# Second products of a convolution and two-layer MLP kernel: the two 64-row halves issued in opposite phase

## The chip, the cores and the metric

The kernel runs on one core of a Trainium2 chip. The metric is the device time of one execution in microseconds, lower is better; a number given as the time of a kernel is the median of several runs.

## What is computed

A dynamic convolution (each of 8 heads mixes 7 neighbouring tokens with softmax weights) makes 16384 tokens of 192 values. They go through an MLP with a squared ReLU:

```python
h = x @ w_in                 # (16384, 192) @ (192, 2048)
r = np.maximum(h, 0.0)
g = s * (r * r) + b
return (g @ w_out)           # (16384, 2048) @ (2048, 192)
```

The kernel is held to float32 inputs and outputs. It splits each operand of a product into a high part that TensorE multiplies exactly (type `fp32r`) and a low part, and adds up the products hi x hi, hi x lo and lo x hi.

## The kernel before

The tokens are cut into 32 groups of 512 (`g`), the 2048 hidden units into four quads of four 128-unit blocks (`k`), so there are 128 stages `n = 4 g + k`. Each stage has first products (`h = x @ w_in` for one quad, into the PSUM tiles `ph`), a squared ReLU on ScalarE (`relu2`: L443, L445, and L449 which writes the high part `gh`), the low part `gl` on VectorE (`low_g`, L455), and second products (`g @ w_out`, into the four PSUM tiles `po`, one for each 128 tokens). ScalarE and VectorE work on stage n while TensorE runs the second products of stage n-1, and VectorE also does the convolution of a later group. When the four quads of a group are summed, VectorE scales the result (L512, L518) and SyncE stores it.

The first four stages run while the weights are still being prepared, and use matmuls over all 128 rows (`mm1_pair`, L408 and L414; `mm2_pair`, L482). From then on every matmul uses 64 rows: `HALVES` (L378) are rows 0 to 63 and 64 to 127 of the contraction, each on one half of the array, with their own weights, so that two matmuls run beside each other. First products are in `mm1_quad` (L432), 36 matmuls of 512 columns a stage. Second products are in `mm2_quad` (L500), 64 matmuls a stage, called 123 times.

In a second product the stationary operand (the weights that are loaded into the array) is 128 tokens of `gh` or `gl`, and the moving one is a row block of `w_out`. With `part` 0 (`gh`) it is w_out's high and low part side by side, 384 columns; with `part` 1 (`gl`) it is the high part alone, 192 columns, added onto the second half of the same PSUM tile (`second`, the two `return dict` lines). `mm2_quad` takes four steps (`at`); in a step the first half of the rows adds to one `po` tile and the second half to another (`first`), so that the halves never write one tile at the same time. Within a step the loop over `c` runs over two 256-unit pairs (`p`), the two blocks in each (`j`) and the two parts, and the innermost loop over the halves:

```python
for c in range(8):
    p, j, part = c // 4, c // 2 % 2, c % 2
    for i, rows in enumerate(HALVES):
        m = second(n, p, j, first[i], part, rows)
```

So both halves are at their 384-column matmul together, then both at their 192-column matmul. The order of a queue is the order of the program (`tc.manual_schedule()`); nothing is reordered by a planner. After each of the first two steps `hand_over` puts a no-op of GpSimd behind the two tiles.

Of the kernel before, what the change touches and what calls it, by code (L numbers as in the profile page):

```python
# [20 lines left out]
def dynamic_conv_then_relu2_mlp(  # L21
# [44 lines left out]
    NQ = M // QUAD  # L66
# [170 lines left out]
    def w2(i, j, rows=slice(0, P)):  # L237

        return wc[i][rows, :, CO + j * D:CO + (j + 1) * D]
# [138 lines left out]
    HALVES = slice(0, 64), slice(64, P)  # L378
# [5 lines left out]
    def hand_over(*sums):  # L384


        for o in sums:
            nc.gpsimd.keepalive_nop(ins=[nc.gpsimd.lower_ap(o)])
# [69 lines left out]
    def outputs(g):  # L458
        o_t[g] = [ps_o.tile([P, 2, D], F32, tag=f"o{t}", name="po") for t in range(NT)]
        y_t[g] = yp.tile([P, NT, D], F32, tag="y", name="y")  # L460

    def second(n, p, j, t, part, rows=slice(0, P)):

        g, k = divmod(n, NQ)
        o, w = o_t[g][t], w2(2 * k + p, j, rows)
        v = g_t[n, p][part][rows, j, t * P:(t + 1) * P]
        start = part == 0 and (g, t) not in begun
        begun.add((g, t))
        if part == 0:
            return dict(out=o, lhsT=v, rhs=w, start=start, stop=False)  # L470
        return dict(out=o[:, 1, :], lhsT=v, rhs=w[:, 0, :], start=False, stop=False)
# [14 lines left out]
    def mm2_quad(n):  # L486


        g, k = divmod(n, NQ)
        if g not in o_t:  # L490
            outputs(g)
        turn = [(0, 2), (2, 0)][::1 - n % 2 * 2]
        for at in range(4):
            first = [a + at % 2 for a in turn[at // 2]]
            for c in range(8):
                p, j, part = c // 4, c // 2 % 2, c % 2
                for i, rows in enumerate(HALVES):
                    m = second(n, p, j, first[i], part, rows)
                    m["stop"] = k == NQ - 1 and at >= 2 and c == 7
                    nc.tensor.matmul(**m)  # L500
            if at < 2:
                hand_over(*[o_t[g][t] for t in first])
        for p in range(2):
            g_t.pop((n, p))
# [29 lines left out]
    with tc.manual_schedule():  # L534
# [22 lines left out]
        for i in range(NC):  # L557
            n, p = divmod(i, 2)
# [25 lines left out]
        for n in range(NQ, last + 1):  # L584
            g, k = divmod(n, NQ)
            if k == 0 and g + 2 < NG:
                load(g + 2)
            if k == 3:
                zeros_before(g + 2)
            mm1_quad(n)  # L590
            relu2(n)
            if n == NQ:
                mm2_pair(n - 1, 1)
            else:
                mm2_quad(n - 1)
            a = (3, 5), (5, 8), (9, 14), (0, 2)
            run_pieces(g + 1 + k // 3, *a[k])
            low_g(n, 0)
            if k == 0:
                scale(g - 1, (0, 2, 1, 3))  # L600
                store(g - 1, 0, NT)
            low_g(n, 1)
            a = (5, 5), (8, 9), (14, 15), (2, 3)
            run_pieces(g + 1 + k // 3, *a[k])
# [36 lines left out]
```

## Time and profile before

| what | value |
|---|---|
| time, median of 3 runs | 1181.46 us (1181.32 to 1181.98) |
| span of the profiled execution (first to last instruction) | 1178.3 us |
| median of the runs less that span | 3.2 us |
| TensorE matmul / weight load busy | 97% / 88% |
| VectorE / ScalarE / GpSimd busy | 80% / 70% / 1% |
| DMA, mean over the span | 43 GB/s |

The profile is of one execution. PE is TensorE's matmul row, PEld its weight loads, DVE is VectorE, ACT ScalarE, POOL GpSimd, SP SyncE. Ends of matmuls are modelled and matmuls overlap, so the time that one takes is read from the distance between starts. Stretches are in microseconds from the start of the span. The profiled execution's own time outside its span is not recorded; the runs' median stands for it in the table.

### The profile page before, as it was taken

Reading aid. Unit: us, or ns where it says so; the run is one execution under the profiler, and the core shown is the slowest. Engines: PE = TensorE matmul, PEld = TensorE weight load, DVE = VectorE, ACT = ScalarE, POOL = GpSimd, SP = SyncE. Lnnn points to the kernel's source line nnn. Section 1 sums busy time; section 2 is a strip of 40 time slices with the busy share of each in tenths; the row PEclk is TensorE's granted clock in tenths of the full one; section 3 lists DMA queues with packets and bytes.
Section 4 is the critical chain, followed back from the end, with each engine's and each line's share of the span. In section 5 each row is a group of like instructions: output and inputs, shape, how many; then the busy total and the mean of one; then the engine's idle time right before and its main releaser. Section 6 shows DMA issues by size and latency. Waiting matters only on the chain.

```text
span 1178.3 us, 29855 instructions
## 1 busy us (share of the span) xinstructions
PE 1144.9 (97%) x12672; PEld 1034.5 (88%) x12672; DVE 938.2 (80%) x1357; ACT 826.4 (70%) x889; POOL 6.1 (1%) x22
## 2 busy tenths in 40 slices
PE   2999999999999999999999999999999999999997
PEld 1678999999999999999999999999999999999997
DVE  7988887788887778887778898777788777888843
ACT  2767767777677677776776776767767677677674
POOL 0000000000000000000000000000000000000000
PEclk9999999999999999999999999999999999999999
DMA  7421222221122222122222112222112222212110
GB/s 155 117 44 28 40 46 47 32 46 27 35 46 46 39 40 37 30 40 47 46 33 46 26 36 46 46 35 44 29 37 42 47 46 33 45 26 36 24 24 14
DMA packets 175833, 50.17 MB, mean 43 GB/s; under 512 B 165076, under 2 KB 168660, under 8 KB 175700
## 3 DMA queue, kind: packets, MB, share of 16 engines
q1 hardware_dynamic: 172820, 47.73, 22.6%
q8 instruction: 99, 1.62, 0.6%
q10 hardware_dynamic: 2880, 0.54, 0.3%
q14 instruction: 34, 0.28, 0.1%
HBM read 27.26 MB, written 12.58 MB: 34 GB/s over the span
## 4 chain that ended last, share of the span: by engine, by line
PE 95%; DVE 2%; ACT 1%; DMA 1%; SPq 0%; issue 0%
PE po L500 47%; PE ph L432 43%; PE po L482 2%; PE ph L219 1%; PE ph L408 1%; DVE pr L300 1%; PE ph L414 1%; DMA r<-in_moe_w_in_dram 0%; DVE gl L455 0%; DVE pr L311 0%; ACT gh L449 0%; PE ph L246 0%; ACT r L445 0%; SPq L101 0%; DMA xb<-xb 0%
## 5 line engine op out<-in xcount | busy, mean ns | idle before, releaser
L500 PE MATMUL po<-wc,gh 64*128 64x384 f32 x3936 | 570.5, 356 | 0.0
L500 PE MATMUL po<-wc,gl 64*128 64x192 f32 x3936 | 492.8, 247 | 0.8 <-DVE gl L455 0.8
L455 DVE TENSOR_TENSOR gl<-r,gh 128x1024 fp32r<-128x1024 f32 x256 | 313.1, 1223 | 213.1 <-ACT gh L449 206.9
L443 ACT ACTIVATE r<-ph 128x1024 f32<-128x1024 f32 x256 | 249.0, 1024 | 300.0 <-PE ph L432 295.1
L500 PEld LDWEIGHTS po<-wc,gl 64*128 64x128 f32 x3936 | 375.7, 188 | 6.3 <-DVE gl L455 1.1
L500 PEld LDWEIGHTS po<-wc,gh 64*128 64x128 f32 x3936 | 368.7, 184 | 5.1
L432 PE MATMUL ph<-xa,wc 64*128 64x512 f32 x2976 | 365.6, 391 | 0.0
L432 PEld LDWEIGHTS ph<-xa,wc 64*128 64x128 f32 x2976 | 269.8, 184 | 52.9 <-issue 0.2
L449 ACT CAST gh<-r 128x1024 fp32r<-128x1024 f32 x256 | 269.2, 1052 | 7.9
L445 ACT ACTIVATE r<-r 128x1024 f32<-128x1024 f32 x256 | 270.7, 1057 | 0.3
L300 DVE TENSOR_TENSOR pr<-xt,w 128x1152 f32<-128x1152 f32 (+1 forms) x128 | 193.6, 1554 | 2.5 <-DMA r<-in_moe_w_in_dram 0.7
L432 PE MATMUL ph<-xb,wc 64*128 64x512 f32 x1488 | 190.4, 388 | 0.0
L432 PEld LDWEIGHTS ph<-xb,wc 64*128 64x128 f32 x1488 | 139.9, 184 | 30.5
L311 DVE TENSOR_TENSOR pr<-pr 128x768 f32<-128x768 f32 (+1 forms) x128 | 145.2, 1155 | 2.1
L512 DVE SCALAR_TENSOR_TENSOR u<-po,s_sb,bias 128x192 f32<-128x192 f32 x128 | 49.8, 410 | 1.6 <-PE po L482 1.6
L518 DVE SCALAR_TENSOR_TENSOR y<-po,s_sb,u 128x192 f32<-128x192 f32 x128 | 49.8, 409 | 0.1
L219 PE MATMUL ph<-r,eye_f 128*128 128x384 f32 x32 | 15.6, 570 | 18.2 <-DVE r L198 18.2
L319 DVE TENSOR_TENSOR acc<-pr 128x768 f32<-128x768 f32 x32 | 30.6, 958 | 1.1
L330 DVE STREAM_TRANSPOSE xT<-acc 128x128 f32<-128x128 f32 x128 | 28.5, 280 | 1.1
L335 DVE STREAM_TRANSPOSE xT<-acc 128x128 f32<-128x128 f32 x128 | 27.2, 271 | 0.0
L482 PE MATMUL po<-wc,gh 128*128 128x384 f32 x80 | 23.9, 361 | 0.1
L219 PEld LDWEIGHTS ph<-r,eye_f 128*128 128x128 f32 x32 | 5.7, 205 | 20.8 <-issue 20.8
(45 smaller groups left out, 336.0 us busy)
## 6 DMA issues: line engine op xcount, KB each, us to landing
xt<-in_x_dram SPq DMA_DIRECT2D x120, 132.0 KB, 3.4
out_dram<-y SPq DMA_DIRECT2D x128, 96.0 KB, 1.9
xb<-xb SPq DMA_DIRECT2D x128, 64.0 KB
wg<-in_weight_gen_dram SPq DMA_DIRECT2D x128, 28.0 KB, 2.6
r<-in_moe_w_out_dram SPq DMA_DIRECT2D x8, 384.0 KB, 3.7
r<-in_moe_w_in_dram SPq DMA_DIRECT2D x16, 128.0 KB, 3.0
r<-in_moe_w_in_dram SPq DMA_DIRECT2D x32, 32.0 KB, 2.2
xt<-in_x_dram ACTq DMA_DIRECT2D x4, 132.0 KB, 4.0
```

What stands on the lines that cost most here:

```text
L219: nc.tensor.matmul(out=o, lhsT=eye_f, rhs=fv[:, c], start=True, stop=False)
L300: nc.vector.tensor_tensor(out=pr[:, k0:k1, :, h * G:(h + 1) * G], in0=bass.AP(xs.tensor, xs.offset, [xs.ap[0], [FQ, n], [FQ, J], [1, G]]), ...
L311: nc.vector.tensor_tensor(out=pr[:, o:o + n], in0=pr[:, o:o + n], in1=pr[:, a:a + n], op=ALU.add)
L432: nc.tensor.matmul(out=h_t[n, p][:, j], lhsT=w1(2 * k + p, part, block, j, rows), rhs=v[rows], start=(at < 2 and c == 0), stop=(at >= 4 an ...
L443: nc.scalar.activation(out=r[p], in_=h_t.pop((n, p)), func=AF.Relu)
L445: nc.scalar.activation(out=r[p], in_=r[p], func=AF.Square)
L449: nc.scalar.copy(out=gh, in_=r[p])
L455: nc.vector.tensor_tensor(out=gl, in0=sq, in1=gh.bitcast(F32), op=ALU.subtract)
L482: nc.tensor.matmul(**m)
L500: nc.tensor.matmul(**m)
L512: nc.vector.scalar_tensor_tensor(out=u[i], in0=o_t[g][tiles[i]][:, 1, :], scalar=s_sb, in1=bias, op0=ALU.mult, op1=ALU.add,)
L518: nc.vector.scalar_tensor_tensor(out=y[:, t], in0=o_t[g][t][:, 0, :], scalar=s_sb, in1=u[i - 1], op0=ALU.mult, op1=ALU.add,)
```

## The change

In `mm2_quad` the loop over `c` goes over the four blocks (`p`, `j`), and the four matmuls of a block are written out with their half `i` and their `part`. Before, their order was half 0 part 0, half 1 part 0, half 0 part 1, half 1 part 1. After, it is half 0 part 0, half 1 part 1, half 1 part 0, half 0 part 1, so that each half has 384 columns while the other has 192. Where a sum is begun (`opens`: the first quad of a group, steps 0 and 1, block 0) the old order is kept, since the 384-column matmul has to clear the PSUM tile first. `stop` marks the last matmul of each half in the new order.

```diff
-            for c in range(8):
-                p, j, part = c // 4, c // 2 % 2, c % 2
-                for i, rows in enumerate(HALVES):
-                    m = second(n, p, j, first[i], part, rows)
-                    m["stop"] = k == NQ - 1 and at >= 2 and c == 7
+            opens = k == 0 and at < 2
+            for c in range(4):
+                p, j = c // 2, c % 2
+                for i, part in ((0, 0), (1, 1), (1, 0), (0, 1)) if c or not opens else ((0, 0), (1, 0), (0, 1), (1, 1)):
+                    m = second(n, p, j, first[i], part, HALVES[i])
+                    m["stop"] = k == NQ - 1 and at >= 2 and c == 3 and part == 1 - i
                     nc.tensor.matmul(**m)
```

## Rows read from the trace of the kernel before

**Rows 1.** Page, engine totals (busy us, share of the span, instructions) and L500's groups

```profile
PE 1144.9 (97%) x12672; PEld 1034.5 (88%) x12672; DVE 938.2 (80%) x1357; ACT 826.4 (70%) x889; POOL 6.1 (1%) x22
...
L500 PE MATMUL po<-wc,gh 64*128 64x384 f32 x3936 | 570.5, 356 | 0.0
L500 PE MATMUL po<-wc,gl 64*128 64x192 f32 x3936 | 492.8, 247 | 0.8 <-DVE gl L455 0.8
```

**Rows 2.** Page, chain that ended last: share of the span by engine, by line

```profile
PE 95%; DVE 2%; ACT 1%; DMA 1%; SPq 0%; issue 0%
PE po L500 47%; PE ph L432 43%; PE po L482 2%; PE ph L219 1%; PE ph L408 1%; DVE pr L300 1%; PE ph L414 1%; DMA r<-in_moe_w_in_dram 0%; DVE gl L455 0%; DVE pr L311 0%; ACT gh L449 0%; PE ph L246 0%; ACT r L445 0%; SPq L101 0%; DMA xb<-xb 0%
```

**Rows 3.** Waits of PE: waiter <- releaser, us in total, times, longest

```profile
PE po L482 <- DVE gl L455: 1.7, 2, 0.9
...
PE po L500 <- DVE gl L455: 0.8, 1, 0.8
```

**Rows 4.** Stage table: stretch, length, busy us (instructions) by engine, granted clock, DMA

```profile
599.67:603.83 4.16, 4.16 (x42) 3.41 (x39) 3.29 (x6) 2.49 (x4) 0.00 (x0) 1.00 0.04 6
603.83:608.39 4.56, 4.56 (x67) 4.56 (x64) 1.05 (x1) 4.50 (x6) 0.00 (x0) 1.00 0.42 63
```

**Rows 5.** Timeline, PE, one quad's second products (start us, length us, operation, count)

```profile
603.83 0.34 PE L500 MATMUL po<-wc,gh 64*128 64x384 f32 x2
604.00 0.25 PE L500 MATMUL po<-wc,gl 64*128 64x192 f32 x2
604.09 0.36 PE L500 MATMUL po<-wc,gh 64*128 64x384 f32 x2
604.29 0.25 PE L500 MATMUL po<-wc,gl 64*128 64x192 f32 x2
604.38 0.36 PE L500 MATMUL po<-wc,gh 64*128 64x384 f32 x2
...
608.10 0.36 PE L500 MATMUL po<-wc,gh 64*128 64x384 f32 x2
608.30 0.25 PE L500 MATMUL po<-wc,gl 64*128 64x192 f32 x2
608.39 1.11 PE L432 MATMUL ph<-xa,wc 64*128 64x512 f32 x8
```

**Rows 6.** Timeline, PEld, start of the same quad

```profile
604.00 0.19 PEld L500 LDWEIGHTS po<-wc,gh 64*128 64x128 f32 x2
604.11 0.19 PEld L500 LDWEIGHTS po<-wc,gl 64*128 64x128 f32 x2
604.29 0.19 PEld L500 LDWEIGHTS po<-wc,gh 64*128 64x128 f32 x2
604.40 0.19 PEld L500 LDWEIGHTS po<-wc,gl 64*128 64x128 f32 x2
604.58 0.19 PEld L500 LDWEIGHTS po<-wc,gh 64*128 64x128 f32 x2
604.69 0.19 PEld L500 LDWEIGHTS po<-wc,gl 64*128 64x128 f32 x2
```

**Rows 7.** Timeline, PE, after the last quad

```profile
1166.56 0.44 PE L482 MATMUL po<-wc,gh 128*128 128x384 f32 x1
1166.84 0.25 PE L482 MATMUL po<-wc,gl 128*128 128x192 f32 x1
```

**Rows 8.** Timeline, PEld, the same place (in brackets: idle before, releaser)

```profile
1166.56 0.19 PEld L482 LDWEIGHTS po<-wc,gh 128*128 128x128 f32 x1 [0.16 <-ACT r L445]
```

**Rows 9.** Timeline, PE, first phase, second products over all 128 rows

```profile
48.62 0.36 PE L482 MATMUL po<-wc,gh 128*128 128x384 f32 x1
48.82 0.25 PE L482 MATMUL po<-wc,gl 128*128 128x192 f32 x1
48.91 0.36 PE L482 MATMUL po<-wc,gh 128*128 128x384 f32 x1
...
50.34 0.36 PE L482 MATMUL po<-wc,gh 128*128 128x384 f32 x1
```

**Rows 10.** Timeline, PE, the wait in the first quad

```profile
98.72 0.36 PE L500 MATMUL po<-wc,gl 64*128 64x192 f32 x2 [0.83 <-DVE gl L455]
```

## The prediction

> **What bounds the kernel now.** I read the page's engine totals first: TensorE's matmul row is busy 97% of the span and no other computing engine passes 80% [rows 1]. The chain that ended last is TensorE for 95%, and one line, the second products of L500, carries 47% of it [rows 2]. The waits of the matmul row show that little is lost to other engines there: L500 waited once, 0.8 us, for a `gl` [rows 3]. So the question is how fast TensorE gets through L500's own stream. The stage table has a regular beat: 4.16 us of first products, 4.56 us of second products, at granted clock 1.00 [rows 4]. There are 123 quads of second products (3936 matmuls of each width, 32 of each a quad [rows 1]), so 123 x 4.56 = 561 us hang on the change.
>
> **One period, read from starts.** Durations of single matmuls overlap, so I go by starts. A row "x2" holds the two halves, which start within 0.01 us of each other (the merged row is as long as one matmul). In a quad the 384-column pairs start at 604.09, 604.38, ... 608.10: 14 periods in 4.01 us, 0.2865 us each [rows 5]. In one of them the 192-column pair starts 0.20 after the 384-column pair, and the next 384-column pair 0.085 after that (0.08 or 0.09 in the rows). But the first 384-column pair, whose weights had been loaded long before, is followed after only 0.17 (603.83 to 604.00), and the first period takes 0.26 (603.83 to 604.09). So about 0.0265 us of every later period is not streaming.
>
> The weight loads say what it is [rows 6]. In the steady quad a half's load starts with its 192-column matmul (604.00, 604.29, 604.58), and its next load 0.11 later (604.11, 604.40, 604.69), although the 384-column matmul between them is taken up already 0.085 after the first load began. So a load occupies its half for 0.11 us (its recorded length, 0.19, is longer than the distance to the next one, so I go by starts here too); the 192-column matmul covers only 0.085 of it, and the 384-column matmul behind it gets its weights 0.025 late. The same is seen where nothing covers a load: after an idle gap at 1166.56 a load and its 384-column matmul have the same recorded start, and the next matmul follows 0.28 later, 0.11 of load and 0.17 of streaming [rows 7, 8]. A matmul's recorded start is therefore when it is taken up, not when its weights are in.
>
> Decisive for the change is whether this stall belongs to each half by itself or to both together, through a common load path. Both halves' loads run side by side and take 0.11 [rows 6]; and in the first phase, where one 128-row matmul has the array to itself (L482), the period is the same: 48.62 to 50.34, six periods in 1.72 us, 0.287 [rows 9]. One load at a time buys nothing there. So I take the stall to be private: in each half, a 384-column matmul behind a 192-column one waits for its own load.
>
> **The change part by part.** Nothing is added or removed: 64 matmuls and 64 loads a quad, 32 of each width, same operands, and the two halves write different PSUM tiles before and after. Only the order of issue moves: of each four, first half 384, second half 192, second half 384, first half 192. No DMA and no other engine's instruction is moved past. Each half still alternates 384 and 192, so each still has one badly covered load a period.
>
> I follow both halves from the start of the first half's 384 at time 0, by the lengths above. Second half: its 192 also at 0; the load for its 384 starts with that and is in at 0.11; its 384 streams until 0.287 (0.176 long behind a late load: 0.2865 - 0.11). First half: its 192 at 0.176, where the next load starts; that is in at 0.287, and the next 384 streams from there. The second half's next 192 needs a load that stands behind the first half's in the program: issued just after 0.176, in at 0.287, which is just when its 384 ends. Period 0.287 for both, as before: 123 x 16 = 1968 periods x (0.2865 - 0.2865) = 0.
>
> That tie is the first unseen cost: the second half's 192 may come some ns late. It then trails and is tied no longer, so the cost falls once a quad, not once a period. No row shows unequal matmuls side by side; what the rows show of a 384 in two surroundings is 0.176 (late load) against 0.17, so I let up to 0.004 us a period stand in doubt either way, 1968 x 0.004 = 8 us. I take 0, by the row of the lone stream [rows 9], which is nearest to two halves that don't touch each other, and keep -8 and +8.
>
> The border of a quad is the second. Before, both halves end on a 192. After, the first half ends on its 192 at 0.26 and the second on its 384 at 0.287; the 512-column matmul that follows in the first half is taken up 0.09 after the 192, as before [rows 5], but has its load in only 0.11 after it, also at 0.287. So the border is a tie too and I cost it at nothing; its cover is that late load. Without the cover one half waits for the other's 384, at most 0.20: 123 x 0.20 = 24 us, the upper end.
>
> Where a new sum opens (one quad in four, first two steps) the old order is kept for the first four matmuls; the second half then runs two 192s in a row, in a slot in which it would have had a 384. Nothing.
>
> `gl` is wanted one matmul earlier, 0.17 us. Only the first quad ever waited for it [rows 3]; that wait, up to 98.72 [rows 10], now also holds back the second half's 384, +0.2 us once. Behind it stands only TensorE's own stream.
>
> Sum: the profiled span 1178.3 + 0.2, and 3.2 us around it (the median 1181.46 less the span): 1181.7, which I round to **1181.6 us**, no change.
>
> **Rivals.** *Ends in program order (slower).* All pairs in the rows are of equal length [rows 5], so nothing shows a short matmul leaving before a longer one that was issued ahead of it. If it isn't let go, each of a period's two slots lasts as long as its 384 (the loads are then covered): 2 x 0.17 = 0.34. Price (0.34 - 0.2865) x 1968 = 105 us: 1287 us. It decides as soon as the second half's 384 is taken up 0.17 instead of 0.085 after its 192. For it: the rows have starts in program order throughout. Against it: in every row each half waits for its own load and stream only. Chance 0.12. The Trainium skill, "TensorE: Matmul & The Clock Gate", Part 3, states this rule, that matmuls keep program order in both start and end, from traces of packed matmuls; by it the change would lose those 105 us, and no row here tests it with unequal lengths.
>
> *The halves are coupled at borders (slower).* One waits for the other up to the 24 us above, or some ns a period: 1184 to 1205. Against it the ties of the walk. 0.15.
>
> *The load path is common (faster).* If the 0.11 is two 64-row loads sharing one path, setting the halves apart could bring the weights of a 384 in time: period 0.26, gain 0.0265 x 1968 = 52 us, 1129 us. For it: half loads have never run alone here. Against it: the lone 128-row stream has the same 0.287 [rows 9], and by the walk the loads still go out in pairs (at 0 and at 0.176). 0.08.
>
> *A few ns a period are won (faster)*, because streams of unequal phase disturb each other less: up to the 8 us above, 1173 to 1179. 0.13.
>
> *The order makes no difference*, the forecast: 0.52.
>
> **How the numbers follow.** A measurement of this kernel can tell about 0.2%, 2.4 us, from no change; that is 1.2 ns a period. Same 0.52; faster 0.08 + 0.13 = 0.21; slower 0.12 + 0.15 = 0.27. The range leaves out the two far cases (0.12 + 0.08 = 0.20) and goes from 8 us under to 24 us over: 1173 to 1205.
>
> **What the profile of the changed kernel would show.** If I am right: quads of 4.56 us in the stage table; in each half 384-column starts 0.287 apart; the second half's 384 taken up 0.085 after its 192; loads still in pairs. Ends in program order: quads of about 5.4 us, and the second half's 384 never less than 0.17 after its 192. A common load path: 384-column starts 0.26 apart, quads of about 4.15 us. Coupled borders: periods of 0.287, but clearly more than 0.09 between the last second product and the first 512-column matmul.

## The result, and the profile of the changed kernel

The changed kernel takes 1188.6 us (median of 4 runs, 1186.8 to 1189.4) against 1181.7 us before: ratio 1.0055, 95% interval 1.0041 to 1.0070. So it is slower, by some 6.9 us. In some executions TensorE's clock rises to full for good some 7 us later than in others, which costs some 2 us, so the medians mix both kinds; the fastest execution on record took 1179.7 us before and 1186.8 after.

The two profiles differ in this. L221 multiplies 384 columns in the first phase; before (first two lines) it takes 0.53 us, the lower of the two clock levels, at 21.90 and 0.33 at 33.74, while in the changed kernel (third line) it still takes 0.52 at 36.96, where the granted clock is 0.5 until 38.2:

```profile
21.90 0.53 PE L221 MATMUL ph<-v,eye 128*128 128x384 f32 x1
33.74 0.33 PE L221 MATMUL ph<-v,eye 128*128 128x384 f32 x1
```

```profile
36.96 0.52 PE L221 MATMUL ph<-v,eye 128*128 128x384 f32 x1
```

(A stage table prints a clock of 1.00 for the first 30 us of the kernel before, but its trace has no clock record ahead of 31.2; the lengths decide.) That is 2.4 of the 9.4 us between the two spans (1178.3 and 1187.7): the first quad of second products starts at 99.36 instead of 96.98. The rest lies in the stages.

The page of the changed kernel, engine totals, chain and L501's groups (L501 is L500 of before), answers to [rows 1, 2]:

```profile
PE 1154.0 (97%) x12672; PEld 1122.2 (94%) x12672; DVE 937.9 (79%) x1357; ACT 826.0 (70%) x889; POOL 6.1 (1%) x22
...
PE po L501 47%; PE ph L432 44%; PE po L482 2%; PE ph L219 1%; PE ph L408 1%; DVE pr L300 1%; PE ph L414 1%; DMA r<-in_moe_w_in_dram 1%; DVE gl L455 0%; DVE pr L311 0%; ACT gh L449 0%; PE ph L246 0%; ACT r L445 0%; SPq L101 0%; PE ph L221 0%
...
L501 PE MATMUL po<-wc,gh 64*128 64x384 f32 x3936 | 626.6, 356 | 0.0
L501 PE MATMUL po<-wc,gl 64*128 64x192 f32 x3936 | 577.9, 248 | 0.8 <-DVE gl L455 0.8
```

The mean of one matmul has hardly moved (356 and 248 ns), and the only wait on VectorE is the 0.8 us of before. The busy sums are larger because two matmuls that ran beside each other now overlap less, which says nothing of the time.

One steady stage in the stage table, first products and then second products by the starts of the half that leads, answers to [rows 4] (4.16 and 4.56 there):

```profile
605.01:609.21 4.20, 4.20 (x41) 4.11 (x39) 3.35 (x6) 2.44 (x5) 0.00 (x0) 1.00 0.00 0
609.21:613.79 4.58, 4.58 (x67) 4.58 (x64) 1.00 (x2) 4.55 (x5) 0.00 (x0) 1.00 0.51 72
```

From the first matmul of one quad to that of the next, the stage takes 8.720 us before and 8.775 after (mean of 100 stages in the trace). 0.055 x 122 = 6.7 us: this is the loss. Most of it, 0.04 of 0.055, is in the first products, whose code the change doesn't touch.

The timeline within a quad of the changed kernel (start us, length us, operation), answers to [rows 5]; now the two halves are rows of their own:

```profile
603.00 0.36 PE L501 MATMUL po<-wc,gh 64*128 64x384 f32 x1
603.09 0.25 PE L501 MATMUL po<-wc,gl 64*128 64x192 f32 x1
603.17 0.36 PE L501 MATMUL po<-wc,gh 64*128 64x384 f32 x1
603.21 0.24 PE L501 MATMUL po<-wc,gl 64*128 64x192 f32 x1
603.29 0.36 PE L501 MATMUL po<-wc,gh 64*128 64x384 f32 x1
603.37 0.25 PE L501 MATMUL po<-wc,gl 64*128 64x192 f32 x1
603.46 0.36 PE L501 MATMUL po<-wc,gh 64*128 64x384 f32 x1
```

One half is 603.00 (384), 603.21 (192), 603.29 (384); the other 603.09 (192), 603.17 (384), 603.37 (192), 603.46 (384). Each has the 0.287 us period, with 0.20 after a 384 and 0.085 after a 192, as before. The border to the first products:

```profile
604.92 0.25 PE L501 MATMUL po<-wc,gl 64*128 64x192 f32 x1
605.01 0.41 PE L432 MATMUL ph<-xa,wc 64*128 64x512 f32 x1
605.09 0.25 PE L501 MATMUL po<-wc,gl 64*128 64x192 f32 x1
605.18 0.36 PE L501 MATMUL po<-wc,gh 64*128 64x384 f32 x1
605.26 2.84 PE L432 MATMUL ph<-xa,wc 64*128 64x512 f32 x22
...
609.21 0.33 PE L501 MATMUL po<-wc,gh 64*128 64x384 f32 x1
609.34 0.39 PE L432 MATMUL ph<-xb,wc 64*128 64x512 f32 x1
```

All 64 second products stand ahead of the first products in the program, yet at 605.01 a matmul of L432 starts ahead of two of L501, and at 609.21 a second product starts ahead of the last first product. The halves are streams of their own: the first half leads the second by 0.36 us, one matmul and more, and keeps that lead from stage to stage.

With the matmuls of L432 put to their halves one by one, by the order of the program, the starts in a stage are these (mean of 100 stages):

```
                        first matmuls of the stage (gaps, ns)            mean of 15 later ones
before, both halves     255 226 233 236 229 232 226 229 232 ...          229.7
changed, leading half   253 226 233 236 229 236 259 236 234 ...          230.9 without the 259
changed, trailing half  232 233 233 233 233 233 233 233 233 ...          233.3
```

The trailing half takes 0.2333 for a 512-column matmul where before both took 0.2297: 18 x 0.0036 = 0.065 us a stage, less 0.01 that its second products gain (16 periods of 0.2862 instead of 0.2867). That is the 0.055. (By starts alone, as in the stage table, 0.04 of it falls on the first products and 0.015 on the second: before, a half's first 512-column matmul comes behind a 192 and gets its weights late, a gap of 255 among the first products, while the trailing half has 232 there and one more late load among its second products.)

The leading half isn't slow by itself; it is held, as by the gap of 259. What holds it is `hand_over`, which `mm1_quad` calls too: behind each of its first two steps a no-op of GpSimd waits for both halves' matmuls of that step, and the first load of the third and of the fourth step (the 7th and the 10th matmul of a half) waits for the semaphore that GpSimd raises. The trace has the times (us):

```
                       3rd matmul of the    GpSimd raises    load for the 7th matmul     load behind the    load behind the
                       later half, start    the semaphore    of the leading half         semaphore          6th matmul
before (at 582.23)     582.713              583.174          583.411                     0.237              0.003
changed (at 587.46)    588.289              588.747          588.790                     0.043              0.155
```

With the halves together the semaphore has been up for 0.24 us when it is wanted. In the changed kernel the trailing half's third matmul comes so late that the leading half's load waits for it, in each of 100 stages looked at, and is 0.155 behind its usual place.

### The profile page after: what moved, and what is told of

Read it like the earlier page. It is cut to its first block, busy times and chain, and to the rows that moved or that the text cites. A ratio compares the mean times of both kernels' runs of the same rounds, so it can differ in the third digit from the quotient of the medians.

```text
span 1187.7 us, 29855 instructions
## 1 busy us (share of the span) xinstructions
PE 1154.0 (97%) x12672; PEld 1122.2 (94%) x12672; DVE 937.9 (79%) x1357; ACT 826.0 (70%) x889; POOL 6.1 (1%) x22
## 4 chain that ended last, share of the span: by engine, by line
PE 95%; DVE 2%; ACT 1%; DMA 1%; SPq 0%; issue 0%
PE po L501 47%; PE ph L432 44%; PE po L482 2%; PE ph L219 1%; PE ph L408 1%; DVE pr L300 1%; PE ph L414 1%; DMA r<-in_moe_w_in_dram 1%; DVE gl L455 0%; DVE pr L311 0%; ACT gh L449 0%; PE ph L246 0%; ACT r L445 0%; SPq L101 0%; PE ph L221 0%
## 5 line engine op out<-in xcount | busy, mean ns | idle before, releaser
L501 PE MATMUL po<-wc,gh 64*128 64x384 f32 x3936 | 626.6, 356 | 0.0
L501 PE MATMUL po<-wc,gl 64*128 64x192 f32 x3936 | 577.9, 248 | 0.8 <-DVE gl L455 0.8
L501 PEld LDWEIGHTS po<-wc,gh 64*128 64x128 f32 x3936 | 575.0, 184 | 0.2
L501 PEld LDWEIGHTS po<-wc,gl 64*128 64x128 f32 x3936 | 555.9, 186 | 1.3 <-DVE gl L455 1.1
L432 PE MATMUL ph<-xa,wc 64*128 64x512 f32 x2976 | 411.3, 394 | 0.0
L432 PEld LDWEIGHTS ph<-xa,wc 64*128 64x128 f32 x2976 | 348.8, 185 | 13.1 <-issue 0.2
L432 PE MATMUL ph<-xb,wc 64*128 64x512 f32 x1488 | 233.5, 390 | 0.0
L432 PEld LDWEIGHTS ph<-xb,wc 64*128 64x128 f32 x1488 | 196.1, 185 | 0.8
```

What stands on the lines that cost most here:

```text
L432: nc.tensor.matmul(out=h_t[n, p][:, j], lhsT=w1(2 * k + p, part, block, j, rows), rhs=v[rows], start=(at < 2 and c == 0), stop=(at >= 4 an ...
```

## The experiments

Four questions, in this order: is it the opposite order itself, the border, or the halves being out of step; does the state stay; what of the second products' end makes a half slow; and what distance does to it. In the diffs, `order` stands for the four (half, part) of a block, `OLD` is ((0,0), (1,0), (0,1), (1,1)) and `NEW` is ((0,0), (1,1), (1,0), (0,1)). Unless said otherwise the steps that open a sum keep their first block in the old order, as in the change.

**One opposite block a quad, and one in the whole kernel.**

```diff
-order = OLD
+order = NEW if at == 3 and c == 3 else OLD                   # e1
+order = NEW if n == NQ + 4 and at == 3 and c == 3 else OLD   # e2
```

> The kernel before, with the opposite order only in the last of the 16 blocks of each quad of second products. Theory A (out of step: the halves lose their common start and then every 512-column first product takes 0.2333 us instead of 0.2297, 18 of them a stage in each half): nearly the whole loss, 1186 to 1189 us, and the first products' starts 0.233 apart from the first quad on. Theory B (the opposite order itself costs 3 to 4 ns in each block of the second products): a sixteenth of the loss, 0.4 us, 1182 us, first products as before. Theory C (the border: the second half ends on a 384-column matmul and the other waits): about 1188 us, but first products 0.2297 apart and the time lost at the border.

> The kernel before, with the opposite order in one single block, the last of the fifth quad of second products, and nowhere else. Theory A: if nothing brings the halves back into step, 118 later stages run at 0.2333 and the time is 1186 to 1188 us; if they fall back into step by themselves, 1181.8. Theories B and C: no difference that can be measured, 1181.7 us (0.054 us at most).

Measured: 1180.8 us, ratio 0.9995 (0.9986 to 1.0004), and 1181.8 us, ratio 0.9998 (0.9989 to 1.0008). Stages are 8.720 us long in both. In e1 the first products take 0.2297 in the first half and 0.2291 in the second, the second half ends every quad on a 384, as in the change, and nothing is lost: the timeline of its border leads straight into a merged row of L432, and by the starts the second half's first 512-column matmul is 0.026 us behind the first half's, the next one 0.001:

```profile
607.91 0.36 PE L502 MATMUL po<-wc,gh 64*128 64x384 f32 x1
607.91 0.27 PE L502 MATMUL po<-wc,gl 64*128 64x192 f32 x1
608.02 0.36 PE L502 MATMUL po<-wc,gh 64*128 64x384 f32 x1
608.11 0.25 PE L502 MATMUL po<-wc,gl 64*128 64x192 f32 x1
608.19 1.34 PE L432 MATMUL ph<-xa,wc 64*128 64x512 f32 x10
```

So theory C (the border) falls, and the tie that the prediction's walk found at the border is there: 0.085 from the first half's last 192 to its first 512, and both halves at one point a matmul later. One block doesn't put the halves out of step for good; theory A lives only if it takes more blocks.

**A common point each stage.** Two first products over all 128 rows instead of four over 64, in the kernel before (control) and in the changed one:

```diff
+if c == 0 and at in (0, 2):
+    for u in (0, 2) if at == 0 else ():
+        nc.tensor.matmul(out=h_t[n, u % 2][:, u // 2], lhsT=w1(2 * k + u % 2, part, 0, u // 2, slice(0, P)),
+                         rhs=v, start=True, stop=False)
+    continue
```

> The kernel before, with two of the first products of each stage over all 128 rows ahead of the others, in place of four over 64 rows: the same streaming, but a matmul over all rows has to wait for both halves and brings them to a common point. It is the control for the next kernel. Two changes of tiling a stage cost some 0.1 to 0.3 us each: 1181.7 plus 25 to 75 us.

> The changed kernel with the same two first products over all 128 rows. Theory A: the halves start every stage's first products in step again, these are 0.2297 apart, and the difference to the control shrinks from 6.7 us to within 1.5 us. Theory B: the order still costs its 6.7 us on top of the control. Theory C: 6.7 us or more on top of the control, lost just ahead of the first matmul over all rows.

Measured: 1229.5 us (ratio 1.0405, 1.0389 to 1.0421) and 1232.6 us (1.0427, 1.0411 to 1.0443). The stages are 9.120 and 9.133 us: the difference between the two orders falls from 0.055 to 0.013 us a stage, 1.6 us over the kernel (the medians differ by 3.1, the profiled spans, 1228.6 and 1230.8, by 2.2). Three quarters of the loss go when the halves are brought together ahead of the first products. Theory B (a price in each block) would have kept all of it. In the traces neither half of e4 runs at 0.2333 (0.2305 and 0.2308 on the mean). The control isn't clean, though: behind its 128-row matmuls one half takes 0.232 to 0.234 for six matmuls, in the old order, so the slow pace is not bound to the opposite one.

**How long the state lasts, and what undoes it.**

```diff
-order = NEW
+order = NEW if n < NQ + 10 else OLD    # e5: first ten quads
+order = NEW if at < 3 else OLD         # e6: three steps of four
+order = NEW if k == 3 else OLD         # e7: one quad in four
```

> The changed order in the first 10 of the 123 quads of second products only, the old order in all later ones. In the changed kernel's trace the distance between the halves grows over the first eight stages and stays. Theory A1 (out of step, and the state stays by itself once it is there): later stages keep first products of 0.233 and the time is about 1187 us. Theory A2 (out of step, and the old order brings the halves back): first products of 0.2297 again a stage or two after the tenth quad, 1182 us. Theory B (the order itself costs in each block): 10/123 of 6.7 us, 1182.2 us, first products never slower.

> The changed order in the first three of the four steps of each quad, the old order in the last step, that is in the four blocks ahead of the first products. Theory A2: four blocks of the old order bring the halves back before the first products begin, these take 0.2297, and most of the loss goes: 1182 to 1183.5 us. Theory A1: the halves stay apart, 1187 to 1189 us. Theory B: three quarters of the loss, 1186.7 us, with first products at 0.2297.

> The changed order in whole quads, but only in the last of each group of four. Theory A2: the stage after such a quad has first products a little over 0.2297, by up to 0.03 us a stage as in the changed kernel's first stages, the other three stages take 8.72 us; 1181.7 to 1182.6 us in all. Theory A1: all stages slower, 1187 us. Theory B: 31 quads at 0.054, 1.7 us, lost in the second products.

Measured: 1182.3 us (ratio 1.0010, 1.0000 to 1.0020), 1181.6 us (1.0000, 0.9990 to 1.0009), and 1184.3 us (one run). The lengths of successive stages, in ns by the leading half's starts, with the distance of two neighbouring starts of L432 in brackets:

```
e5  stages 6 to 9        8787 8773 8782 8772     first products, trailing half: 233.3
    stages 10 to 16      8753 8739 8743 8731 8735 8754 8717     229.7
    stages 17 on         8720 8720 8720 ...      229.7 [210/20]
e6  stages 1 to 19       8720 8720 8720 ...      229.7 both, [163/66] ... [117/113] ... [17/213]
e7  stages 4 to 6        8719 8721 8719          233.3 in one half in stage 4 only, then 229.7 [57/173]
    from stage 16 on     8733 on the mean
```

Three things follow. The old order ends the slow first products in the very next stage (e5: 0.2297), and the distance that has piled up is paid back over six stages. With three quarters of all blocks in opposite phase there is no loss at all (e6), which theory B had at 1186.7. And in e6 the second half drifts from 0.163 us behind the first to some 0.18 ahead, where it stays, with first products at 0.2297 on the way: being apart is not what slows them, and theory A falls in the form in which I stated it. What e7 shows is that one half is slow in the stage right behind an opposite quad, and that this costs nothing (8.72 us) until the half has fallen far enough behind.

**Who is issued first.** The changed kernel with the first products in the order second half, first half:

```diff
-for i, (block, u) in enumerate(step):
+for i, (block, u) in list(enumerate(step))[::-1]:
```

> The changed kernel, with the first products issued second half first. In the changed kernel the first half runs about one matmul ahead of the second. If the order of issue is what lets it, the lead is cut or turned round at each stage's first products and the loss changes clearly (1182 to 1186 us, or more than 1190); if the distance comes from the second products' order alone, 1188 to 1189 us as with the change.

Measured: 1188.1 us, ratio 1.0064 (1.0049 to 1.0079), stages of 8.775. The order of issue of the first products doesn't matter.

**How a half ends its quad.** Three endings:

```diff
-order = NEW
+order = ((0,1), (1,1), (0,0), (1,0)) if at == 3 and c == 3 else OLD   # e9: in step, both end on 384
+order = OLD if at == 3 and c == 3 else NEW                            # e10: opposite, both end on 192
+order = ((0,1), (1,0), (0,0), (1,1))                                  # e11: roles exchanged
```

> The old order, but in the last block of each quad both halves do 192 first and 384 last, so that both go into the first products from a 384-column matmul, with the load of their first 512-column matmul covered; nothing is in opposite phase. Theory H2 (a half that comes out of a 384, its next load covered, runs the stage's 512-column matmuls at 0.2333): both halves slower by 18 x 0.0036 us a stage, 1189 us. Theory H3 (a half does so only if it also stands apart from the other, since the half that ended on a 384 beside the other in the kernel with one opposite block a quad ran at 0.2291): 1181.6 us, 512-column starts 0.2297 apart.

> The changed kernel, with the old order in the last of the 16 blocks of each quad, so that both halves go into the first products from a 192-column matmul; 15 blocks stay in opposite phase. Theories H2 and H3: both halves at 0.2297 and most of the loss gone, 1181.5 to 1183 us. Theory H4 (the distance that fifteen opposite blocks build up is what slows the first products; four old blocks had been enough to undo it): 1186 to 1188 us, the second half's 512-column starts 0.2333 apart.

> Opposite phase with the roles exchanged: of each four, first half 192, second half 384, first half 384, second half 192, so that the first half ends on a 384 and the second on a 192. Theories H2 and H3: now the first half's 512-column starts are 0.2333 apart, and the time is that of the change, 1187 to 1189 us. Theory H5 (the second half is the slower one because it stands second in the program): the first half stays at 0.2297 and the time is 1182 to 1185 us.

Measured: 1182.0 us (0.9999, 0.9989 to 1.0009), stages of 8.720, first products at 0.2291: a covered first load in both halves does no harm where they stand together, so H2 falls. 1180.0 us (0.9986, 0.9977 to 0.9996), stages of 8.718, first products at 0.2297: fifteen of sixteen blocks in opposite phase and the loss is gone, so H4 falls. With stages as long as before, the 0.14% ahead is no gain of the order. And 1187.8 us (1.0054, 1.0036 to 1.0071) with the roles exchanged, where it is now the first half, the one that ends on a 384, that runs at 0.2333: H5 falls.

The exchange also shows how the loss comes about, since it starts from halves in step. Gaps of L432 in its fourth stage of 64-row matmuls, and the lengths of the stages:

```
leading half (second)   229 231 226 229 232 226 229 231 227 229
trailing half (first)   233 234 233 234 233 233 234 233 233 234
distance of the halves  22, 75, 129, 183 ns in four stages running
stages (leading half)   8720 8720 8720 8746 8747 8798 8735 8739 8775 ... mean 8775
```

A stage from that stretch, and one from the middle:

```profile
111.38:120.10 8.72, 8.72 (x105) 8.72 (x102) 4.33 (x7) 6.94 (x8) 0.00 (x0) 1.00 0.26 37
593.77:602.51 8.74, 8.74 (x104) 8.65 (x102) 8.15 (x15) 5.91 (x7) 0.00 (x0) 1.00 0.01 2
```

The trailing half loses 0.054 us a stage from the start. For three stages the leading half goes on at 8.720, and the distance grows by just these 54 ns a stage. When the trailing half is some 0.23 us behind, the leading half begins to be held, and from there on both take the trailing half's time. The place is again `hand_over`, which had 0.24 us to spare: in each of 100 stages of e8, e11 and e12, as of the change, the leading half's loads for its 7th and 10th matmul start 0.041 to 0.046 us after GpSimd has raised the semaphore. No run leaves `hand_over` out or moves it.

**Apart, and both ending on a 384.**

```diff
-order = NEW
+order = ((0,1), (1,1), (0,0), (1,0)) if at == 3 and c == 3 else NEW
```

> The changed kernel, with the last block of each quad in the order 192, 192, 384, 384, so that both halves go into the first products from a 384-column matmul; the 15 blocks ahead of it stay in opposite phase, so the halves stand apart. Theory H3a (a half runs its 512-column matmuls at 0.2333 if it comes from a 384 and stands apart from the other): both halves at 0.2333, 1187 to 1190 us. Theory H3b (it does so only where the other half comes from a 192, that is, where the two endings are unequal): both at 0.229 to 0.230 and 1180 to 1182.5 us.

Measured: 1189.0 us, ratio 1.0068 (1.0052 to 1.0085), stages of 8.775. The time is H3a's, but only the trailing half, which did 192, 384 in the last block and in those ahead of it, runs at 0.2333; the leading half, which also ended on a 384, has gaps of 226, 229 and 232 with a few where it is held. So H3a isn't the rule either. Two stages of this run put a narrower light on it: in its third stage of 64-row matmuls the trailing half starts 176 ns behind the leading one and takes 232, 236, 229, 232; in the fourth it starts 180 ns behind and takes 232, 233, 233, 234.

**What stands and what stays open.** Shown: the loss is 0.0036 us on each 512-column first product of one half; in every kernel that loses it is a half that has done 192 and then 384 up to the end of the quad (the second half in the change, e8 and e12, the first in e11); one block in the old order at the end removes it; the other half follows because `hand_over` lets it get no further ahead. It needn't be all sixteen blocks: in the quads that open a sum the first and the fifth block are in the old order, and the stage behind them is as slow. So the last eleven are enough and the last one alone is not (e1, e9, the leading half of e12); no run tells where between them the line lies.

Not shown: why that half's matmuls then start every 0.2333 instead of in the pattern 0.226, 0.229, 0.232. It isn't the distance of the halves: the full rate is seen in e6 from 0.163 us behind to 0.17 ahead and in e5, on the way back, from 0.35 to 0.21 behind, and in e11 the trailing half keeps 0.2333 while the distance goes from 0 to 0.22. Nor does the order alone decide. The third stages of the change and of e5 have the same program behind them; in the one the trailing half runs at 0.2333, 0.189 us behind, in the other at 0.2289, 0.198 behind. A few nanoseconds in how a half enters the stage would fit this and the last two lines on e12; no run here moves them by so little on purpose.

## Why the prediction was right and where it was wrong

The forecast was no change, 1181.6 us, with 1173 to 1205 as the range and 0.27 on slower; 1188.6 us lies in the range, on the side of the rival of coupled halves (1184 to 1205), which had 0.15. That the range holds it is luck: its upper end was the price of a wait at the border, which doesn't occur, and the loss came from a place that the range wasn't made for.

Each half's stall behind its own load: right. The period of the second products, on which 561 us hung, is 0.2862 us for the trailing half, which sets the pace, against the 0.2865 of the forecast, with the load still 0.11 and the 384 late by 0.025. This is also why the idea behind a common load path found nothing to gain, and that rival (1129 us) has fallen: quads near 4.15 us, its mark, don't occur. In the changed kernel the loads still go out in pairs, 0.003 to 0.012 us apart, as the forecast had it; e5 tests the rival without them: from its stage 17 on the halves' loads are 0.03 to 0.10 us apart, and the period is 0.2867.

The second half's 384 is taken up 0.085 after its 192 (603.09 and 603.17), so the rival of ends in program order (1287 us) fell at its own mark. More than that: matmuls of the two halves don't even start in program order, as 605.01 ahead of 605.09 shows. The sentence of the Trainium skill that I weighed there, "TensorE: Matmul & The Clock Gate", Part 3, doesn't hold here; the trace decides.

The border as a tie, cost nothing: right. e1 has the border of the change in every quad and takes 8.720 us a stage.

The step that failed is one that the prediction didn't write down as a term: that the first products, 18 matmuls a half and 4.16 us a stage, stay as they are. Its sum went over the second products, their two borders and `gl`. The wait for `gl` was indeed 0.8 us. The missing term is 18 x 0.0036 = 0.065 us a stage, 8 us over the kernel, of which the second products gave 0.01 a stage back. The second slip is near it: "it then trails and is tied no longer, so the cost falls once a quad". It overlooked `hand_over` in the first products: once the trailing half is some 0.2 us behind, the leading half waits there for it, in every stage, and then all that the one loses is lost by both.

The rival that was nearest had the sign and the size (up to 24 us or some ns a period), but its place was wrong: it put the price at the border or in the second products. By its own mark, periods of 0.287 but more than 0.09 between the last second product and the first 512-column matmul, it would have been turned down, since that distance is 0.085 (604.92 to 605.01).

The uncertainty of 0.004 us a period that I allowed for unequal neighbours is close to the 0.0036, but by chance: it was meant for the second products, whose period stayed, and the loss fell on the 512-column matmuls.

## What to carry to other kernels

Where two halves of the array run their own streams, a stall that belongs to one stream (here a 0.11 us load behind a 0.085 us matmul) isn't cured by shifting the streams against each other; first look whether a lone stream has the same period. A change of order in one stage can slow a later stage whose code is untouched, so the sum has to have a line for each stage that shares the engine, if only with a bound. And where one stream loses a few ns a stage, look how far the other may run ahead, and which wait in the program sets that: until then the loss doesn't show in the time, after that it shows in full.

## What the runs showed of the hardware that I had not expected

Matmuls on different row halves start out of program order: the leading half was 0.36 us ahead, with matmuls of L432 running while two of L501 that stand ahead of them had not begun. In the kernels that lose, what bounds the lead is the program's own `hand_over` (held from 0.23 us on in e11, steady at 0.36 in the change). The Trainium skill, "TensorEngine Tiling (Array Packing)", Tiling Modes, says that different tiles can run their loads and matmuls in parallel, independently of each other; the drift in e6 from 0.163 us behind to 0.17 ahead, with first products at 0.2297 on the way, agrees.

The start-to-start time of a 512-column matmul isn't one number at full clock: in long stretches it is either a cycle of 0.226, 0.229 and 0.232 us or a steady 0.2333, both at granted clock 1.00. The means 0.2291 and 0.2297 are the same cycle with other gaps in the first few matmuls of the stage.
